# A fused retention and squared-ReLU feed-forward kernel: the last group of tokens moved to the seven-product form and woven into the group in front, and one operand sum rebuilt from another

## The chip, the cores and the metric

The kernel runs on one core of one Trainium2 chip. The metric is device time in microseconds (us) for one execution. The engines are written as in the profile: PE (matrix multiply), PEld (its weight load, which runs ahead of the multiply), DVE (vector), ACT (scalar and activations), POOL (GpSimd), SP (the queue that issues nearly all DMAs).

## What is computed

The reference, cut to what matters:

```python
B, H, S, D = 8, 8, 576, 64             # q, k, v: [B, H, S, D] float32
scores = q @ k.T / sqrt(D)
ret    = (scores * Dmat) @ v           # Dmat: gamma_h ** (i - j) for i >= j, else 0
x      = ret.transpose(0, 2, 1, 3).reshape(B * S, 512)   # 4608 tokens x 512
h      = x @ w_in                      # w_in  512 x 2048
g      = relu(h) ** 2
out    = g @ w_out                     # w_out 2048 x 512, float32
```

## The kernel before

**Tiles and groups.** The 4608 tokens are 36 units of 128 tokens; two units make a group, so there are 18 groups, numbered 0 to 17 (`groups`, line 132 on). The last group holds its two units in reverse order. A unit is a chunk of 128 positions of one batch, or a "tail", the last 64 positions of two batches together.

**Stages of one unit.** k, q and v are loaded in float32 by DMA, cast to float16 by POOL, k and q are transposed (by PE for the first eight units, by DMA after), and the retention is worked out in 64 x 64 pieces on PE (`psc` scores, `psS` running sums, `psO` outputs). DVE writes the result as `xT`, the operand of the feed-forward part.

**Feed-forward of one group, first product** (`add_ff`, line 805 on). `ph = x @ w_in` comes in eight blocks of 8 matmuls of 128x256 (64 matmuls; 4 matmuls make one slice of 128 hidden features, and a block holds two slices). ACT takes each block through Relu into `rl` (line 827), then ACT (`SQ_ACT`: blocks 0 to 6) or DVE (block 7; in groups 0 and 1 all blocks) squares it into `gT` (lines 837, 839).

**Second product.** Groups 0, 1 and 17 use the plain form (line 860). The other fifteen (`STRASSEN = 2`) use `add_strassen` (line 878 on), Strassen's scheme in Winograd's form on 2 x 2 blocks: seven block products of 8 matmuls of 128x256 in place of eight, that is 56 matmuls in place of 64 such, or of 32 matmuls of 128x512. The four quarters of g are G(s, i): s is the unit (A or B), i the lower or upper half of the hidden features. DVE forms four sums in float16, each in two halves h0 and h1, into `gS` (line 890):

- S3 = G(A,0) - G(B,0), S1 = G(B,0) + G(B,1), S2 = S1 - G(A,0), S4 = G(A,1) - S2.

The order of the products on PE is P1, P7, P6, P2, P5, P3, P4. P7 reads S3, P6 reads S2, P5 reads S1, P3 reads S4; P1, P2, P4 read g itself. P1, P6, P5 and P3 add up in one PSUM bank "a", and ACT copies its state out after P1, P6 and P5 (line 925) and after P3 (line 955). P7 and P4 share bank "c". DVE adds the copies to banks and writes the output tile `o` (line 935). SP stores it.

**Names in the trace.** In rows of line 912 (all seven products) `po<-w_out,gT` is P1 or P2, `po<-wT,gS` is P7, P6 or P5, `po<-w_out,gS` is P3 and `po<-wT,gT` is P4. `wT` are differences of `w_out` blocks, made once by DVE (line 772).

**What sets the order.** All work is entered as tasks with an engine, a key, a duration and what it depends on (`Schedule`, line 16 on). `emit` walks through time with these durations, gives each free engine the ready task of the smallest key, and so fixes the order of the instructions on each engine once and for all. On the chip an engine works in this order and waits when an operand isn't there. The planner also counts buffers: `ff=4` PSUM banks for `ph` and `po`, `rl=3`, `u` buffers `p1`, `u2`, `u4` one each. Where `p6`'s operand is late in the plan, the planner puts first-product work of the next group ahead of it.

**Loads at the start.** `FIRST` gives the order of the first loads: pairs of units (`k0`, `q0`, ...) and eight weight blocks of 1 MB (`w0` to `w3` of w_in, `w4` to `w7` of w_out), one after the other on SP (`add_load_pair`, line 284; `add_weight`, line 295). The planner takes a load as landed 2.1 us after its slot ends.

**The end.** Group 17's plain second product is 16 matmuls of 128x512 for one unit, then 2 x 16 of 128x256 for the other. ACT copies each result out (line 869) and issues the stores itself (`store`, line 786).

Of the kernel before, what the change touches and what calls it, by code (L numbers as in the profile page):

```python
# [9 lines left out]
FP32 = mybir.dt.float32  # L10
FP16 = mybir.dt.float16
ACTF = mybir.ActivationFunctionType
ALU = mybir.AluOpType
# [88 lines left out]
def kernel(  # L102
# [9 lines left out]
    nc = tc.nc  # L112
    B, H, S, D = q.shape
    DM, DFF = w_in.shape
    assert (B, H, S, D, DM, DFF) == (8, 8, 576, 64, 512, 2048)
    P = 128
    NP = H // 2
    NF = DFF // P
# [13 lines left out]
    groups = []  # L132
# [16 lines left out]
    u_pool = ctx.enter_context(tc.tile_pool(name="u", bufs=1))  # L149
# [75 lines left out]
    SQ_ACT = (0, 1, 2, 3, 4, 5, 6)  # L225
    JOIN = 11
    PAIRED = 8
    FIRST = ["k0", "q0", "v0", "k2", "q2", "w0", "v2", "w1", "w2", "w3", "w4", "w5", "w6", "w7", "k4", "q4", "v4", "k6", "q6", "v6"]
    sched = Schedule(dict(ff=4, prS=1, prO=1, g=3, ld=5, wst=4, kq=7, v16=7, rT=4, x=3, rl=3, o=4, p1=1, u2=1, u4=1,
# [32 lines left out]
    def dma_task(key, dur, fn, **kw):  # L262
        t = add("SP", key, dur, fn, deps=list(last_load), **kw)
        last_load[:] = [t]
        return t
# [18 lines left out]
    def add_load_pair(name, u):  # L284
        b, c = units[u][1:]
        n = "kqv".index(name)

        def fn():
            if name != "q":
                tile_of["stage", u] = stage.tile([P, 2, H, 2 * D], FP32, name="pair", tag="wst")  # L290
            x = tile_of[name + "32", u] = tile_of["stage", u][:, n % 2]
            nc.sync.dma_start(out=x, in_=(k, q, v)[n][b, :, c * P:(c + 2) * P, :].rearrange("h (p e) d -> p h (e d)", e=2))
        loaded[name, u] = loaded[name, u + 1] = dma_task(0, 1.81 if loaded else 2.9, fn, acq=("wst",) if name != "q" else ())

    def add_weight(i):
# [10 lines left out]
        t = dma_task(0, 2.75, fn, acq=("wst",))  # L306
# [479 lines left out]
    def store(u, o, lo=0, hi=DM):  # L786
        kind, b, c = units[u]

        eng = nc.scalar if group_of[u] == len(groups) - 1 else nc.sync
        if kind == "full":  # L790
            r0 = b * S + c * P
            eng.dma_start(out=out[r0:r0 + P, lo:hi], in_=o[:, lo:hi])
        else:
            for i in range(2):
                r0 = (b + i) * S + 512
                eng.dma_start(out=out[r0:r0 + 64, lo:hi], in_=o[i * 64:(i + 1) * 64, lo:hi])
# [8 lines left out]
    def add_ff(g):  # L805
        us = groups[g]
        n = len(us)
        base = us[0] * L
# [3 lines left out]
        for fb in range(NF // nf):  # L812
            for j in range(nf):
# [7 lines left out]
                f1.append(add("PE", base + (nf * fb + j) * n, 0.01 + 0.2133 * n, f,  # L821
# [7 lines left out]
            on_act = n == 2 and g >= STRASSEN and fb in SQ_ACT  # L829
# [10 lines left out]
            r = add("ACT", base + 4 * fb + 4, 0.6, fr, deps=[f1[-1]], acq=("rl",))  # L840
            sched.free("ff", [r])
            sq.append(add("ACT" if on_act else "DVE", base + 4 * fb + 6, 0.63 if on_act else 0.45, fg, deps=[r] + sq[:1],
# [4 lines left out]
        if STRASSEN <= g < len(groups) - 1:  # L847
            add_strassen(g, us, base2, sq)
            return
        for s, u in enumerate(us):  # L850
            end = base2 + NF * (s + 1)
            f2 = T["ff2"][-1:] if s == 0 else f2[-1:]

            cuts = [(0, DM)] if u != groups[-1][-1] else [(0, HM), (HM, DM)]
            for ci, (lo, hi) in enumerate(cuts):
                for fi in range(NF):
                    def f(fi=fi, s=s, u=u, lo=lo, hi=hi):
                        if fi == 0:
                            tile_of["po", u, lo] = ps_ff.tile([P, hi - lo], FP32, name="po", tag="ff")
                        nc.tensor.matmul(tile_of["po", u, lo], lhsT=tile_of["g", g][:, fi, s * P:(s + 1) * P],  # L860
                                         rhs=w_out16[:, fi, lo:hi], start=(fi == 0), stop=(fi == NF - 1))
                    f2.append(add("PE", base2 + NF * s + fi / len(cuts) + 8 * ci, 0.0025 + 0.2135 / len(cuts), f,
                                  deps=[sq[fi // nf]] + wcast[4 + fi // 4] + f2[-1:],
                                  acq=("ff",) if fi == 0 else ()))

                def fo(u=u, lo=lo, hi=hi):
                    if lo == 0:
                        tile_of["o", u] = o_pool.tile([P, DM], FP32, name="o", tag="o")
                    nc.scalar.copy(out=tile_of["o", u][:, lo:hi], in_=tile_of["po", u, lo])
                oc = add("ACT", end + 1, 0.12 + 0.47 / len(cuts), fo, deps=[f2[-1]], acq=() if lo else ("o",))  # L870
                sched.free("ff", [oc])
                st = add(*(("ACT", end + 1.1, 0.05) if g == len(groups) - 1 else ("SP", -0.5, 0.7)),
                         lambda u=u, lo=lo, hi=hi: store(u, tile_of["o", u], lo, hi), deps=[oc], after=2.5)
            sched.free("o", [st])
# [3 lines left out]
    def add_strassen(g, us, base, sq):  # L878
        uA, uB = us
# [20 lines left out]
        s1 = add_sum(0, base, lambda h: G(1, 0, h), lambda h: G(1, 1, h), ALU.add, lambda h: low(h) + high(h) + s3[:1])  # L900
        s2 = add_sum(1, base + 1, lambda h: Sx(0, h), lambda h: G(0, 0, h), ALU.subtract, lambda h: [s1[h]])
        s4 = add_sum(3, base + 4, lambda h: G(0, 1, h), lambda h: Sx(1, h), ALU.subtract, lambda h: [s2[h]])
# [36 lines left out]
        p1 = product(1, 0, "a", raw(0, 0), wB[0, 0], low, True, True, [])  # L939
        c1 = on_act_copy("p1", "a", 5, [p1])  # L940
        p7 = product(7, 4, "c", summed(2), wT[2], lambda h: [s3[h]], True, True, [])
        p6 = product(6, 8, "a", summed(1), wT[1], lambda h: [s2[h]], False, True, [c1])
        c2 = on_act_copy("u2", "a", 13, [p6])
        p2 = product(2, 12, "b", raw(0, 1), wB[1, 0], high, True, True, [])
        d11 = on_dve_add(uA, 0, "b", "p1", 17, [p2, c1], ("o",))
        sched.free("ff", [d11])
        sched.free("p1", [d11])
        p5 = product(5, 16, "a", summed(0), wT[0], lambda h: [s1[h]], False, True, [c2])
        c4 = on_act_copy("u4", "a", 21, [p5])
        d22 = on_dve_add(uB, 1, "c", "u4", 22, [p7, c4], ("o",))  # L950
        sched.free("u4", [d22])
        p3 = product(3, 20, "a", summed(3), wB[1, 1], lambda h: [s4[h]], False, True, [c4])

        def f12():
            nc.scalar.copy(out=o_tile(uA)[:, HM:], in_=bank("a"))
        c12 = add("ACT", base + 25, 0.37, f12, deps=[p3, d11])
        sched.free("ff", [c12])
        p4 = product(4, 24, "c", raw(1, 1), wT[3], high, False, True, [d22])
        d21 = on_dve_add(uB, 0, "c", "u2", 29, [p4, d22])
        sched.free("ff", [d21])  # L960
        sched.free("u2", [d21])
# [3 lines left out]
        for u, ds in ((uA, [d11, c12]), (uB, [d22, d21])):  # L965
            st = add("SP", -0.5, 0.7, lambda u=u: store(u, o_tile(u)), deps=ds, after=2.5)
            sched.free("o", [st])
# [44 lines left out]
```

## Time and profile before

| what | value |
|---|---|
| five runs | 297.94, 297.97, 298.6, 299.36, 299.38 us; median 298.6 |
| the profiled execution | 297.97 us, of which the span of the trace is 296.2 us |
| granted PE clock | 1.000 over the span |
| DVE busy | 195.1 us (66%) |
| ACT busy | 187.3 us (63%) |
| POOL busy | 93.3 us (32%) |
| first-product matmuls, line 819 | 1152 |
| seven-product matmuls, line 912 | 840 |
| plain second-product matmuls, line 860 | 112 |

The span is the time from the first to the last instruction of the trace; 1.8 us of the execution lie outside it. A busy PE is a PE with a matmul in its pipeline; consecutive matmuls overlap, so a count of instructions times their mean duration gives more than the time they take. The pace of a stretch is better read from its first and last start. The runs shown lie within 0.5%.

### The profile page before, as it was taken

Reading aid. Unit: us, or ns where it says so; the run is one execution under the profiler, and the core shown is the slowest. Engines: PE = TensorE matmul, PEld = TensorE weight load, DVE = VectorE, ACT = ScalarE, POOL = GpSimd, SP = SyncE. Lnnn points to the kernel's source line nnn. Section 1 sums busy time; section 2 is a strip of 40 time slices with the busy share of each in tenths; the row PEclk is TensorE's granted clock in tenths of the full one; section 3 lists DMA queues with packets and bytes.
Section 4 is the critical chain, followed back from the end, with each engine's and each line's share of the span. In section 5 each row is a group of like instructions: output and inputs, shape, how many; then the busy total and the mean of one; then the engine's idle time right before and its main releaser. Section 6 shows DMA issues by size and latency. Waiting matters only on the chain.

```text
span 296.2 us, 10048 instructions
## 1 busy us (share of the span) xinstructions
PE 286.1 (97%) x4320; PEld 233.8 (79%) x4320; DVE 195.1 (66%) x413; ACT 187.3 (63%) x354; POOL 93.3 (32%) x129
## 2 busy tenths in 40 slices
PE   8989989999999999999999999999999999999995
PEld 3558745688878888888888888788888888888874
DVE  3777469869395949493959597766786767462410
ACT  5357753484867676748576667656666666658861
POOL 4453384434242415063414153414141520000000
PEclk9999999999999999999999999999999999999999
DMA  7999999999999999899979699999898980101012
GB/s 201 326 371 385 363 261 236 195 208 167 209 166 213 178 194 171 203 213 220 163 172 165 156 187 223 201 176 197 155 215 144 216 156 10 73 3 71 2 71 73
DMA packets 139262, 54.14 MB, mean 183 GB/s; under 512 B 118097, under 2 KB 130641, under 8 KB 139217
## 3 DMA queue, kind: packets, MB, share of 16 engines
q1 hardware_dynamic: 138768, 52.97, 86.0%
q8 instruction: 34, 0.56, 0.8%
q10 hardware_dynamic: 448, 0.52, 0.6%
q14 instruction: 12, 0.09, 0.1%
HBM read 36.70 MB, written 9.44 MB: 156 GB/s over the span
## 4 chain that ended last, share of the span: by engine, by line
PE 68%; DVE 10%; ACT 10%; DMA 6%; issue 2%; POOL 2%; POOLq 0%
PE po L912 27%; PE ph L819 26%; ACT rl L827 5%; DVE gS L890 5%; PE psO L337 4%; ACT gT L837 4%; PE po L860 4%; DMA wo<-in_moe_w_out_dram 3%; PE warm L241 3%; DMA pair<-in_k_dram 3%; DVE gT L839 2%; PE psc L337 1%; PE psS L337 1%; PE psT L412 1%; POOL qx L397 1%
## 5 line engine op out<-in xcount | busy, mean ns | idle before, releaser
L819 PE MATMUL ph<-xT,w_in 128*128 128x256 f16 x1152 | 139.3, 273 | 0.0
L819 PEld LDWEIGHTS <-w_in 128*128 128x128 f16 x1152 | 111.2, 98 | 14.8 <-POOL w_in L316 0.3
L827 ACT ACTIVATE rl<-ph 128x512 f16<-128x512 f32 x144 | 84.0, 588 | 52.0 <-PE ph L819 49.1
L837 ACT ACTIVATE gT<-rl 128x512 f16<-128x512 f16 x112 | 70.5, 630 | 3.5
L890 DVE TENSOR_TENSOR gS<-gT 128x512 f16<-128x512 f16 x60 | 31.1, 519 | 40.4 <-ACT gT L837 39.8
L912 PEld LDWEIGHTS <-gS 128*128 128x128 f16 x480 | 45.7, 98 | 9.3 <-DVE gS L890 3.8
L912 PE MATMUL po<-wT,gS 128*128 128x256 f16 x360 | 49.2, 273 | 1.6 <-DVE gS L890 1.2
L361 POOL TENSOR_TENSOR v<-v,vdec_full 128x512 f16<-128x512 f32 x24 | 25.6, 1068 | 56.8 <-DMA v<-in_v_dram 53.8
L912 PEld LDWEIGHTS <-gT 128*128 128x128 f16 x360 | 34.8, 98 | 4.4 <-issue 0.2
L912 PE MATMUL po<-w_out,gT 128*128 128x256 f16 x240 | 31.1, 273 | 0.0
L349 POOL CAST kq<-k 128x512 f16<-128x512 f32 x28 | 19.1, 681 | 34.6 <-DMA k<-in_k_dram 25.6
L839 DVE TENSOR_TENSOR gT<-rl 128x512 f16<-128x512 f16 x32 | 17.7, 555 | 14.2 <-ACT rl L827 13.9
L349 POOL CAST kq<-q 128x512 f16<-128x512 f32 x28 | 18.2, 648 | 26.5 <-DMA q<-in_q_dram 26.1
L860 PE MATMUL po<-w_out,gT 128*128 128x512 f16 (+1 forms) x112 | 22.6, 349 | 0.3 <-POOL w_out L316 0.3
L698 DVE TENSOR_TENSOR xT<-psO,gam_full 128x512 f16<-128x512 f32 x28 | 18.4, 684 | 3.4 <-PE psO L337 3.3
L925 ACT COPY u<-po 128x256 f32<-128x256 f32 x30 | 11.0, 367 | 14.5 <-PE po L912 14.4
L935 DVE TENSOR_TENSOR o<-po,u 128x256 f32<-128x256 f32 x30 | 12.5, 418 | 11.3 <-PE po L912 7.7
L637 DVE TENSOR_TENSOR rT<-psc,mask 128x512 f16<-128x512 f32 x28 | 18.5, 681 | 1.3 <-PE psc L337 1.3
L860 PEld LDWEIGHTS <-gT 128*128 128x128 f16 x112 | 10.6, 98 | 8.1 <-issue 0.5
L890 DVE TENSOR_TENSOR gS<-gT,gS 128x512 f16<-128x512 f16 x30 | 16.3, 546 | 1.0
L890 DVE TENSOR_TENSOR gS<-gS,gT 128x512 f16<-128x512 f16 x30 | 15.8, 527 | 1.0
L912 PE MATMUL po<-wT,gT 128*128 128x256 f16 x120 | 15.8, 273 | 0.2 <-DVE o L935 0.2
(78 smaller groups left out, 263.9 us busy)
## 6 DMA issues: line engine op xcount, KB each, us to landing
out_dram<-o SPq DMA_DIRECT2D x31, 256.0 KB, 3.1
k<-in_k_dram SPq DMA_DIRECT2D x24, 256.0 KB, 4.6
q<-in_q_dram SPq DMA_DIRECT2D x24, 256.0 KB, 5.0
v<-in_v_dram SPq DMA_DIRECT2D x24, 256.0 KB, 4.7
wi<-in_moe_w_in_dram SPq DMA_DIRECT2D x4, 1024.0 KB, 9.9
wo<-in_moe_w_out_dram SPq DMA_DIRECT2D x4, 1024.0 KB, 9.6
pair<-in_k_dram SPq DMA_DIRECT2D x4, 512.0 KB, 4.2
pair<-in_q_dram SPq DMA_DIRECT2D x4, 512.0 KB, 7.3
```

The costliest lines, as they stand in the source:

```text
L337: nc.tensor.matmul(out_, lhsT=lhsT, rhs=rhs, start=start, stop=True, skip_group_check=True, tile_position=(64 * row, 64 * col))
L349: op(out=out_.rearrange("p (n b a d) -> p n b a d", n=2, b=2, a=2), in_=in_.rearrange("p (n a b) d -> p n b a d", n=2, a=2))
L361: nc.gpsimd.tensor_tensor(out=t, in0=tile_of["v32", u], in1=vdec[kind].rearrange("p (h o) -> p h o", o=1).to_broadcast([P, H, D]), op=ALU. ...
L637: nc.vector.tensor_tensor(out=r, in0=tile_of["psc", g][:, :, cols(s)].rearrange("p a (n i) -> p a n i", i=64), in1=mask.rearrange("p (o r ...
L698: nc.vector.tensor_tensor(out=tile_of["x", g][:, :, s * P:(s + 1) * P].rearrange("p n (c i) -> p c n i", c=2), in0=tile_of["psO", g][:, :, ...
L819: nc.tensor.matmul(tile_of["ph", g, fb][:, j, :], lhsT=w_in16[:, m, fi * P:(fi + 1) * P], rhs=tile_of["x", g][:, m, :], start=(m == 0), st ...
L827: nc.scalar.activation(out=t, in_=tile_of["ph", g, fb], func=ACTF.Relu)
L837: nc.scalar.activation(out=t, in_=rl, func=ACTF.Square)
L839: nc.vector.tensor_tensor(out=t, in0=rl, in1=rl, op=ALU.mult)
L860: nc.tensor.matmul(tile_of["po", u, lo], lhsT=tile_of["g", g][:, fi, s * P:(s + 1) * P], rhs=w_out16[:, fi, lo:hi], start=(fi == 0), stop= ...
L890: nc.vector.tensor_tensor(out=Sx(k, h), in0=in0(h), in1=in1(h), op=op)
L912: nc.tensor.matmul(tile_of["pb", g, bank], lhsT=left(i), rhs=right[:, i, :], start=(start and i == 0), stop=(i == HF - 1), skip_group_chec ...
```

## The change

Three things are changed.

1. **S2 from S3.** S2 is now G(B,1) - S3, which is the same value as S1 - G(A,0). It depends on S3 and the upper half, no longer on S1. In the order of the keys S2 comes ahead of S1. This holds for all groups with seven products.
2. **The last group.** Group 17 also uses seven products. Its first product gets keys that put it ahead of the second product of group 16. Its P1, P6, P5, P3 (one quarter of the output) go in parts of two matmuls among the products of group 16 where the planner finds room, and P2, P7, P4 come last. P4 has a bank of its own ("e"), and P7 is first added to a copy (new line 966). Four stores of 128x256 take the place of three: those of d11 and d22 are issued by ACT, those of c12 and d21 by SP. In groups 16 and 17 only blocks 1, 4 and 6 are squared by ACT (`SQ_LATE`), the other five by DVE. The `u` buffers become two each.
3. **The plan's times for four loads.** `LAG` tells the planner that v2, w1, k4, q4 land 1.2, 1.3, 0.7 and 0.5 us later than it assumed. The order of the loads stays; the order of other work on the engines moves.

```diff
-    u_pool = ctx.enter_context(tc.tile_pool(name="u", bufs=1))
+    u_pool = ctx.enter_context(tc.tile_pool(name="u", bufs=2))
...
+    SPREAD = 0.1
+    SQ_LATE = (1, 4, 6)
+    LAG = {"v2": 1.2, "w1": 1.3, "k4": 0.7, "q4": 0.5}
-    sched = Schedule(dict(... p1=1, u2=1, u4=1, ...
+    sched = Schedule(dict(... p1=2, u2=2, u4=2, ...
...
-        loaded[...] = dma_task(0, 1.81 if loaded else 2.9, fn, acq=...)
+        loaded[...] = dma_task(0, 1.81 if loaded else 2.9, fn, acq=..., after=2.1 + LAG.get(name + str(u), 0.0))
-        t = dma_task(0, 2.75, fn, acq=("wst",))
+        t = dma_task(0, 2.75, fn, acq=("wst",), after=2.1 + LAG.get(f"w{i}", 0.0))
...
-        base = us[0] * L
+        base = min(us) * L
+        def place(x):
+            return base + x if g < last_g else base - NF * n - 1 + SPREAD * x
...
-            on_act = n == 2 and g >= STRASSEN and fb in SQ_ACT
+            on_act = g >= STRASSEN and fb in (SQ_ACT if g < last_g - 1 else SQ_LATE)
...
-        if STRASSEN <= g < len(groups) - 1:
+        if STRASSEN <= g:
             add_strassen(g, us, base2, sq)
...
-        s1 = add_sum(0, base, ... G(1, 0, h), ... G(1, 1, h), ALU.add, low(h) + high(h) + s3[:1])
-        s2 = add_sum(1, base + 1, ... Sx(0, h), ... G(0, 0, h), ALU.subtract, [s1[h]])
-        s4 = add_sum(3, base + 4, ...)
+        early = 12 if g == last_g else 0
+        s2 = add_sum(1, base - 4 - early, ... G(1, 1, h), ... Sx(2, h), ALU.subtract, high(h) + [s3[h]])
+        s1 = add_sum(0, base + 1 - early, ... G(1, 0, h), ... G(1, 1, h), ALU.add, low(h) + high(h) + s3[:1])
+        s4 = add_sum(3, base + 4 - early, ...)
...
+        if g == last_g:
+            last[:] = []
+            at = -2 * NF * n
+            p1 = product(1, at + 3.5, "a", raw(0, 0), wB[0, 0], low, True, True, [])
+            c1 = on_act_copy("p1", "a", at + 8, [p1])
+            p6 = product(6, at + 11.5, "a", summed(1), wT[1], lambda h: [s2[h]], False, True, [c1])
+            c2 = on_act_copy("u2", "a", at + 16, [p6])
+            p5 = product(5, at + 19.5, "a", summed(0), wT[0], lambda h: [s1[h]], False, True, [c2])
+            c4 = on_act_copy("u4", "a", at + 24, [p5])
+            p3 = product(3, at + 27.5, "a", summed(3), wB[1, 1], lambda h: [s4[h]], False, True, [c4])
+            c12 = add("ACT", base + 1, 0.37, f12, deps=[p3], acq=("o",))
+            p2 = product(2, 12, "b", raw(0, 1), wB[1, 0], high, True, True, T["ff2"][-1:])
+            d11 = on_dve_add(uA, 0, "b", "p1", 17, [p2, c1, c12])
+            p7 = product(7, 16, "c", summed(2), wT[2], lambda h: [s3[h]], True, True, [])
+            p4 = product(4, 24, "e", raw(1, 1), wT[3], high, True, True, [])
+            d22 = on_dve_add(uB, 1, "c", "u4", 21, [p7, c4], ("o",))
+            d7 = add("DVE", base + 22, 0.42, f7, deps=[d22, c2], acq=("p1",))
+            d21 = on_dve_add(uB, 0, "e", "p1", 29, [p4, d7])
+        else:
...
```

The order of the instructions in the two programs, as the planner fixes it. From the end of P4 of group 15 on, PE has work worth 228 matmuls of 128x256 in the kernel before (a matmul of 128x512 counted as two) and 224 in the changed one; of this, four first-product matmuls of group 16 stood ahead of that point before. Between P7 and the second half of P6, the first-product matmuls that PE has are, for groups 2 to 15: before 12, 12, 12, 12, 12, 12, 12, 12, 20, 16, 16, 16, 12, 12; after 16, 8, 8, 8, 16, 8, 8, 8, 12, 16, 12, 12, 16, 8 (in group 13 with scores and part of the retention outputs of the next group among them). In the first 40 us, eight of the 128 first-product matmuls of groups 0 and 1 move behind the cast of the last weight block. On SP, the loads of the first 60 us keep their order among themselves.

## The prediction

> **What bounds the kernel now.** I read the page first: PE is busy over nearly the whole span, no other engine over 66%.
>
> ```profile
> span 296.2 us, 10048 instructions
> PE 286.1 (97%) x4320; PEld 233.8 (79%) x4320; DVE 195.1 (66%) x413; ACT 187.3 (63%) x354; POOL 93.3 (32%) x129
> ```
>
> The timeline of PE and PEld then gives the pace. From 268.05 us, 44 first-product matmuls take until the next group starts at 272.85: 0.109 us each, and a product of 8 takes 0.87 us. One matmul of 128x512 costs two of these (16 from 285.95, the next half at 289.4). From 262.4 us to the end no row of PE or PEld shows a wait: the end is matmuls, back to back, then one copy and one store. Each work item taken off PE there is time saved.
>
> ```profile
> 285.95 7.11 PE L860 MATMUL po<-w_out,gT 128*128 128x512 f16 x48
> ...
> 291.54 0.37 ACT L869 COPY o<-po 128x256 f32<-128x256 f32 x1 [1.35 <-PE po L860]
> ...
> 293.10 0.37 ACT L869 COPY o<-po 128x256 f32<-128x256 f32 x1 [1.19 <-PE po L860]
> 293.50 0.34 ACTq L792 DMA_DIRECT2D out_dram<-o  x1
> ```
>
> Where does PE wait earlier? The list of waits has one entry that the change touches:
>
> ```profile
> PEld L912 <- DVE gS L890: 3.8, 8, 0.7
> ```
>
> Eight waits of P6 for S2. In the weight-load timeline they stand at 83.00 (0.52 us), 128.01 (0.35), 143.36 (0.58), 187.88 (0.74), 189.43 (0.34), 203.84 (0.50), 218.74 (0.42) and 233.60 (0.38), 3.83 us in all, in groups 3, 6, 7, 10 (twice), 11, 12, 13. PE never makes these up, since everything behind it is dense. The vector timeline of group 7 shows the chain that ends in one:
>
> ```profile
> 140.86 0.43 DVE L839 TENSOR_TENSOR gT<-rl 128x512 f16<-128x512 f16 x1
> 141.32 1.24 DVE L890 TENSOR_TENSOR gS<-gT 128x512 f16<-128x512 f16 x1
> 142.60 0.71 DVE L890 TENSOR_TENSOR gS<-gS,gT 128x512 f16<-128x512 f16 x1
> ```
>
> Square of block 7, then S1, then S2 of half h1, ending 143.31; P6's second half loads at 143.36.
>
> **Part 1, S2 from S3.** It removes S1 from in front of S2; DVE's work stays the same. The price of the removed step: an undisturbed sum takes 0.43 us (median of the rows of line 890), but here it took 1.24, since POOL's v multiply ran from 141.24 to 142.28. This is where the Trainium skill speaks against the change: *SBUF — State Buffer*, "Who interferes with whom", says that a vector instruction with two SBUF inputs is shut out by a GpSimd instruction that reads SBUF, for the whole of that instruction, if that began first. So the delay belongs to POOL's instruction and not to S1: S2, now first, would pay it instead. By the row, S2 is earlier by what S1 took: 1.24 us in group 7, 1.15 in group 6. By the rule S2 now ends about where S1 ended (142.56), earlier by only what S2 itself took: 0.71 us, or 0.43 where POOL is quiet. I take the rule's reading.
>
> Against that: the planner knows S2 is earlier and puts first-product work that filled the gap elsewhere. In groups 3, 7, 10, 12 and 13 PE comes to the second half of P6 with four to eight matmuls fewer since P7, 0.44 to 0.87 us sooner; in group 6 four more; in group 11 as many. Per wait, saved = wait - max(0, wait + sooner - S2's gain):
>
> - group 3: S1 ended at 81.76, S2 at 82.95 (1.15 us); wait 0.52 gone but for some 0.05: saves 0.45
> - group 6: four matmuls more, S2 0.72 earlier: saves 0.35
> - group 7: 0.44 sooner, 0.71 earlier, 0.58 - 0.27 left: saves 0.27
> - group 10: first wait, S2 0.45 to 1.15 earlier but less work in front; second 0.43 earlier; of 1.08 I take 0.4 as saved
> - group 11: same work, 0.43 earlier: saves 0.43
> - group 12: 0.44 sooner, 0.43 earlier: saves 0
> - group 13: scores and outputs of the next group (about 0.9 us) now lie in front: saves 0.38
>
> Sum 2.3 (0.45 + 0.35 + 0.27 + 0.4 + 0.43 + 0.38). The groups without a wait had little or much in hand (S2 ends at 98.11 for a load at 98.16 in group 4, at 112.07 for 112.94 in group 5); with PE 0.44 sooner and S2 0.43 earlier they keep it. I take off 0.3 for small new waits: **2.0 us**, with 0 (each saved gap planned away) and 3.8 (all gone) as the ends. S1 and S4 come later by one step, 0.43 to 0.71 us; P5 and P3 read them one product (0.87) or more behind P6, so that is covered; without P2 in between it would cost its length.
>
> **Part 2, the last group.** 56 matmuls of 128x256 take the place of 64 such: 8 x 0.109 = **0.87 us** off PE, if PE stays dense. I checked the new order with the durations of the rows, T being the end of group 15's P4. All first-product work and P1 of group 16 end by T+13.1. ACT then carries 14 Relus (0.59) and 5 squares (0.63), 11.4 us, in the 12 us from T+1.0: behind by at most 0.7 us; last Relu done at T+13.7, copy of P1 of group 16 at T+14.1. P6 of 16 starts at T+14.8: a reserve of 0.7 us. The last S2 of group 17 needs block 7's square (DVE, T+14.2) and is there at T+14.6; P6's second half at T+16.6. The copies of bank "a" of the two groups alternate, so each (0.37, plus about 0.1 from PE) lies beside 0.87 us or more of the other group's product. Taking squares to DVE costs nothing: 10 x 0.43 + 16 sums x 0.43 + 8 adds x 0.42 = 14.5 us of DVE in 25, and POOL's last row is before 250. Banks: with P1's held, the first product turns over three; block k waits for the Relu of block k-3, done 0.5 us or more ahead. If ACT were over 0.7 us later than this, PE would wait by the excess.
>
> The last step: DVE's add (0.42) for ACT's copy (0.37), +0.05; SP, not ACT, issues the store after a hand-over, about +0.1; SP's stores of 128 KB took a median 2.5 us to land, ACT's 1.7, but SP's ran beside loads and these do not: between 0 and 0.8, I take 0.1. The added d7 follows d22 (0.42 each) after P7 and ends with P4, 0.87 us after P7: 0 to 0.1 more. Splitting the stores in halves puts two more DMAs on the queues, both beside P7 and P4. So the end gains 0.87 - 0.05 - 0.1 - 0.1, **0.6 us**.
>
> **Part 3, the first 60 us.** The loads keep their order and arrive as before, so PE meets the same arrivals with its work in another order. Before, the outputs of group 1 (`psO`, 23.2 us) stood behind 12 first-product matmuls of w1; now they stand behind four. Eight others move ahead of the sums (`psS`) that wait for v2, into PE's 1.34 us before 19.46; but w1's cast ends at 21.73 in any order, and PE had only warm-up matmuls to do up to there, so this gains nothing. At 24 us PE has done 20 first-product matmuls, not 28, and is about 0.35 us ahead for it: 0.5 us behind. It then waits some 0.75 us for w4's cast (29.95), and when w7's is there (38.26) it has eight matmuls, 0.87 us, to do that were done before. What can take them up is idle time that PE had behind that:
>
> ```profile
> 38.32 2.32 PE L860 MATMUL po<-w_out,gT 128*128 128x512 f16 x10 [0.33 <-POOL w_out L316]
> ...
> 41.16 0.40 PE L412 MATMUL psT<-ident,kx 128*128 128x128 f16 x4 [0.30 <-POOL kx L397]
> ...
> 49.06 0.30 PE L337 MATMUL psO<-kqT,R 64*64 64x128 f16 x4 [0.19 <-DVE rx L455]
> ```
>
> The weight loads are idle 0.47 and 0.68 us before the last two and 0.28 before 43.19, 1.4 us in all, most of which the 0.87 us can fill. At 49 us PE waits for DVE's masks, so the time up to there is DVE's. Price: **+0.2 us**; ends -0.6 (the idle time gone) and +1.2 (0.87 in full and a new wait of 0.3).
>
> **Sum.** -2.0 - 0.6 + 0.2 = -2.4 us. The profiled execution took 297.97 (span 296.2), so 295.6 by its own time. It is at the low end of its five runs; from their median, 298.6, the forecast is **296.2 us**.
>
> **The rivals.**
>
> *The planner takes the gain back.* S2 is earlier by 0.43 and PE is sent to it earlier by 0.44, as in group 12, in most groups. For it: ten of the groups 2 to 15 have fewer matmuls in the gap. Against it: four of the seven waiting groups keep the work or get more, or gain over 0.44. Then only -0.6 + 0.2 remain: 298.2, chance 0.23.
>
> *Slower: POOL's multiply falls on S2.* The nine groups with less work in the gap (all those but 13, where scores take its place) have PE there 0.44 us or more sooner. If POOL's v multiply (1.04 us, two to a group of 14.9 us) hits the square of block 7 or S2 there, that is a wait of about 0.6 us: the square took 1.04 instead of 0.43 at 216.43. For it: five of the present waits (81.46, 125.86, 141.24, 186.28, 216.15) have such a row in front, and loads and casts now move against DVE. Against it: S2 stands only one step behind the square now, so fewer steps can be hit. It decides from waits of 5.1 us in all (3.83 + 0.6 - 0.2 + 0.9), 0.37 per group where it is 0.27 now. With 0.6 in the nine and 0.2 in the other five it is 6.4: 298.6 + 2.6 - 0.4 = 300.8. Chance 0.14.
>
> *The end doesn't hold.* ACT is some 1.3 us later than worked out at T+14, so that P6 waits 0.6 us and the gain of the end is gone: 296.8. Chance 0.09.
>
> **Numbers.** Forecast 0.54 (its own range 294.6 to 297.5), taken back 0.23, slower 0.14, end not held 0.09. A difference under 0.3%, 0.9 us, can't be told from none. Faster by more: the forecast but 0.02, the whole last case, a quarter of the second, 0.66. Within: 0.02 and most of the second, 0.19. Slower: the third and 0.01 of the second, 0.15. The low end, 294.4, is 3.8 at P6 and 0.6 at the end with the start as it was, 298.6 - 4.4 = 294.2, nearly in full; the high end, 299.3, takes in the second case with the start at its +1.2 (299.2) and leaves out the slower one, 0.14, and little else.
>
> **What would show it.** Right: PEld's waits for gS fall from 3.8 us to about 1.5; PE is dense behind the last first-product matmul; the last store is issued about 0.6 us after DVE's last add starts. Wrong: waits for gS in groups 3, 7, 10 or 12 as long as now, or new ones with a POOL row on the square or S2; waits of P6 for ACT's copies in the last 12 us; group 2's P1 later than its 63.6 us by more than 0.5.

## The result, and the profile after

The changed kernel takes **297.22 us** (median of 31 runs), the kernel before 298.68 (52 runs); the ratio is 0.9961 with a 95% interval of 0.9949 to 0.9974. That is 1.2 us (0.8 to 1.5) by the ratio, half of the 2.4 that were forecast. The profiled execution of the changed kernel took 297.33 us, at its median; that of the kernel before, 297.97, had been 0.7 under its own. So the two traces differ by less (0.6 us of span) than the medians.

The page of the changed kernel, span and busy times:

```profile
span 295.6 us, 10076 instructions
...
PE 285.8 (97%) x4328; PEld 235.0 (80%) x4328; DVE 204.1 (69%) x433; ACT 183.2 (62%) x347; POOL 94.6 (32%) x129
```

DVE has 9 us more to do, PE nearly the same busy time. The list of waits of the changed kernel (engine, tile and line that waited, what ended the wait: total us, times, longest), the entries of the seven products that end with DVE:

```profile
PEld L914 <- DVE gS L891: 1.9, 6, 0.6
...
PE po L914 <- DVE o L937: 0.9, 3, 0.5
...
PE po L914 <- DVE gS L891: 0.4, 1, 0.4
```

The first entry was 3.8 us, eight times. It fell by 1.9, as forecast. The second is new: P4 waits three times for d22, the add that reads P7 out of the bank that P4 adds to. Group 7 shows how the one became the other. DVE's timeline of the changed kernel (start, us, engine, line, operation):

```profile
141.27 0.42 DVE L891 TENSOR_TENSOR gS<-gT,gS 128x512 f16<-128x512 f16 x1
141.61 1.26 DVE L891 TENSOR_TENSOR gS<-gT 128x512 f16<-128x512 f16 x1
142.80 0.82 DVE L891 TENSOR_TENSOR gS<-gT,gS 128x512 f16<-128x512 f16 x1
...
147.10 1.10 DVE L670 TENSOR_TENSOR R<-stmp,dec 128x256 f16<-128x256 f32 x1
148.13 0.41 DVE L937 TENSOR_TENSOR o<-po,u 128x256 f32<-128x256 f32 x1
```

POOL's:

```profile
141.43 1.16 POOL L365 TENSOR_TENSOR v<-v,vdec_full 128x512 f16<-128x512 f32 x1 [0.81 <-PE psS L341]
...
146.88 1.04 POOL L365 TENSOR_TENSOR v<-v,vdec_full 128x512 f16<-128x512 f32 x1 [1.91 <-DMA v<-in_v_dram]
```

And PE's, with its idle time in brackets:

```profile
148.59 1.03 PE L914 MATMUL po<-wT,gT 128*128 128x256 f16 x8 [0.49 <-DVE o L937]
```

S2 (141.27) is now first and short; S1 behind it takes 1.26, beside POOL's multiply of v. P6 no longer waits. But DVE then works without a break to d22 at 148.13, with a second multiply (146.88) on the last step of R, 1.10 in place of 0.42. In the kernel before, the two rows were

```profile
148.06 0.41 DVE L935 TENSOR_TENSOR o<-po,u 128x256 f32<-128x256 f32 x1
...
148.76 1.05 PE L912 MATMUL po<-wT,gT 128*128 128x256 f16 x8
```

so PE came to P4 after d22 had ended. Now PE is there at 148.10, and waits for a d22 that is as late as it was.

The end of the changed kernel, timeline of all engines:

```profile
291.71 0.41 DVE L966 TENSOR_TENSOR p<-po,u 128x256 f32<-128x256 f32 x1
...
292.23 0.42 DVE L937 TENSOR_TENSOR o<-po,p 128x256 f32<-128x256 f32 x1
292.68 0.34 SPq L794 DMA_DIRECT2D out_dram<-o  x1
```

The last result is ready at 292.65, where the copy had ended at 293.47; SP's hand-over costs 0.03 us. The store then needs 2.9 us to the end of the span, where ACT's needed 2.7. Over the sixteen traces of this document, it is 2.94 to 3.07 us behind SP's last store (nine kernels) and 2.68 to 2.70 behind ACT's (seven).

**Where the time went.** The trace is cut in three at instructions that stand behind the same work in all kernels: the first matmul of P1 of group 2 and of group 15. A **loss** is the time from the start of one matmul to the start of the next, less the median of that time for the same kind of matmul; it is counted where it is over 0.06 us, between these two points. Losses at P6 are for S2 or the sums near it, at P4 for d22, at R for the masked sums that the retention outputs read. The 0.1 that PE loses at each switch to or from retention work, in every kernel, is left out. The three stretches are up to the P1 of group 2, from there to the P1 of group 15, and from there to the end of the span. All in us, from one profiled execution each; e1 to e14 are explained below.

| kernel | ratio to before, 95% | P1 of group 2 | to P1 of 15 | to the end | P6 | P4 | R |
|---|---|---|---|---|---|---|---|
| before | 1 | 63.62 | 195.10 | 37.47 | 2.90 | 0.31 | 0 |
| after | 0.9961 (0.9949 to 0.9974) | 63.89 | 194.75 | 36.97 | 1.18 | 1.16 | 0.16 |
| e1_p1_only | 0.9934 (0.9911 to 0.9958) | 63.61 | 194.58 | 37.46 | 2.15 | 0 | 0.67 |
| e2_p1_held | 0.9896 (0.9865 to 0.9927) | 63.36 | 193.37 | 37.47 | 0.33 | 1.09 | 0 |
| e3_p2_only | 0.9982 (0.9963 to 1.0001) | 63.57 | 196.19 | 37.03 | 3.55 | 0.61 | 0.12 |
| e4_p3_only | 0.9991 (0.9977 to 1.0004) | 63.91 | 194.65 | 37.47 | 2.72 | 0 | 0 |
| e5_p2_own | 0.9990 (0.9972 to 1.0008) | 63.59 | 195.96 | 36.99 | 3.96 | 0 | 0.08 |
| e6_held_own | 0.9887 (0.9861 to 0.9913) | 63.68 | 192.80 | 36.99 | 0.43 | 0.48 | 0 |
| e7_after_held | 0.9874 (0.9844 to 0.9904) | 64.01 | 192.80 | 37.05 | 0 | 0.37 | 0.54 |
| e8_held_vcopy | 0.9859 (0.9829 to 0.9889) | 63.69 | 191.82 | 37.46 | 0 | 0 | 0 |
| e9_after_vcopy | 0.9871 (0.9850 to 0.9893) | 63.82 | 192.09 | 37.10 | 0.25 | 0 | 0 |
| e10_held_vcopy2 | 0.9863 (0.9843 to 0.9884) | 63.73 | 191.92 | 37.07 | 0 | 0 | 0 |
| e11_d22_lag | 0.9931 (0.9909 to 0.9954) | 63.87 | 193.00 | 36.97 | 0.52 | 0 | 0.57 |
| e12_held_d22_lag | 0.9879 (0.9858 to 0.9899) | 63.72 | 192.82 | 36.99 | 0.59 | 0 | 0.29 |
| e13_before_vcopy | 0.9866 (0.9827 to 0.9905) | 63.87 | 192.37 | 37.48 | 0.52 | 0 | 0 |
| e14_before_s2lat | 0.9924 (0.9902 to 0.9947) | 64.32 | 192.65 | 37.48 | 0.07 | 0.78 | 0 |

For the changed kernel the columns read: 1.72 us less at P6, 0.85 more at P4 and 0.16 more at R, so 0.71 less by these; the stretch is 0.35 shorter. The other 0.36 is three steps inside the retention work, which no column has: 0.17 in group 6, where an output at 132.26 follows DVE's masked scores `rT` (ended at 132.21), and 0.11 at 81.17 and 0.08 at 239.22, whose cause is open.

The columns come from single executions, which can lie off their kernel's median: e11's 1.25 us under it, that of e4 and of the kernel before 0.7 under, those of e1 and e3 0.4 over. They show what was waited for; what a kernel costs is read from the ratios.

### The profile page after: what moved, and what is told of

Its sections match the earlier page's. It is cut to its first block, busy times and chain, and to the rows that moved or that the text cites. A ratio compares the mean times of both kernels' runs of the same rounds, so it can differ in the third digit from the quotient of the medians.

```text
span 295.6 us, 10076 instructions
## 1 busy us (share of the span) xinstructions
PE 285.8 (97%) x4328; PEld 235.0 (80%) x4328; DVE 204.1 (69%) x433; ACT 183.2 (62%) x347; POOL 94.6 (32%) x129
## 4 chain that ended last, share of the span: by engine, by line
PE 78%; DVE 8%; DMA 6%; ACT 3%; SPq 2%; issue 2%; POOL 0%; DVEq 0%
PE ph L825 36%; PE po L914 30%; PE po L863 5%; DMA wi<-in_moe_w_in_dram 3%; PE psO L341 3%; DMA wo<-in_moe_w_out_dram 3%; DVE gS L891 2%; SPq L295 2%; PE psc L341 2%; PE psS L341 1%; ACT gT L843 1%; DVE o L937 1%; ACT rl L833 1%; DVE rT L641 1%; DVE stmp L666 1%
## 5 line engine op out<-in xcount | busy, mean ns | idle before, releaser
L843 ACT ACTIVATE gT<-rl 128x512 f16<-128x512 f16 x104 | 65.6, 631 | 3.0
L914 PEld LDWEIGHTS <-gS 128*128 128x128 f16 x512 | 49.1, 98 | 7.7 <-DVE gS L891 1.9
L891 DVE TENSOR_TENSOR gS<-gT,gS 128x512 f16<-128x512 f16 x64 | 38.0, 596 | 21.4 <-ACT gT L843 20.8
L914 PE MATMUL po<-wT,gS 128*128 128x256 f16 x384 | 52.2, 273 | 0.4 <-DVE gS L891 0.4
L891 DVE TENSOR_TENSOR gS<-gT 128x512 f16<-128x512 f16 x64 | 33.4, 522 | 20.5 <-ACT gT L843 20.5
L914 PEld LDWEIGHTS <-gT 128*128 128x128 f16 x384 | 37.3, 98 | 5.4 <-issue 0.9
L914 PE MATMUL po<-w_out,gT 128*128 128x256 f16 x256 | 34.5, 273 | 0.0
L914 PE MATMUL po<-w_out,gS 128*128 128x256 f16 x128 | 16.6, 273 | 0.0
L863 PE MATMUL po<-w_out,gT 128*128 128x512 f16 x64 | 15.6, 379 | 0.5 <-POOL w_out L320 0.4
L670 DVE TENSOR_TENSOR R<-stmp,dec 128x256 f16<-128x256 f32 x24 | 13.3, 553 | 0.7
```

The source lines that it names most:

```text
L843: nc.scalar.activation(out=t, in_=rl, func=ACTF.Square)
L863: nc.tensor.matmul(tile_of["po", u], lhsT=tile_of["g", g][:, fi, s * P:(s + 1) * P], rhs=w_out16[:, fi, :], start=(fi == 0), stop=(fi == N ...
L891: nc.vector.tensor_tensor(out=Sx(k, h), in0=in0(h), in1=in1(h), op=op)
L914: nc.tensor.matmul(tile_of["pb", g, bank], lhsT=left(i), rhs=right[:, i, :], start=(start and i == 0), stop=(i == HF - 1), skip_group_chec ...
```

## The experiments

Two theories stood at first for the missing half. A: DVE's chain is late in any order, and what P6 saves is waited for at d22. B: the planner saw the earlier S2 and spent it.

**Each part alone.**

e1, part 1 in the kernel before:

```diff
-        s1 = add_sum(0, base, ... G(1, 0, h), ... G(1, 1, h), ALU.add, ...)
-        s2 = add_sum(1, base + 1, ... Sx(0, h), ... G(0, 0, h), ALU.subtract, lambda h: [s1[h]])
+        s2 = add_sum(1, base - 4, ... G(1, 1, h), ... Sx(2, h), ALU.subtract, lambda h: high(h) + [s3[h]])
+        s1 = add_sum(0, base + 1, ... G(1, 0, h), ... G(1, 1, h), ALU.add, ...)
```

> The kernel before with part 1 alone (S2 from S3, with its key). The prediction: -2.0 us, as P6's waits for S2 go. Theory A (DVE is what is late): DVE works without a break from the squares through the three sums to d22, its work is no shorter, and what PE saves at P6 it waits for at P4 (for d22) or for R: about -0.4 us, the weight loads' waits for gS down by 2 us and P4's waits for DVE's o up by 0.8. Theory B (the planner): also about -0.4 us, but because first-product work was moved away from in front of P6 and P4; the two are told apart by the next kernel.

e2, the same sums, but the planner isn't told: S2 takes S1's slot, S1 takes that of S2, and in the plan P6 waits for the second slot:

```diff
-        s1 = add_sum(0, base, ...)
-        s2 = add_sum(1, base + 1, ...)
+        s2 = add_sum(1, base, ... G(1, 1, h), ... Sx(2, h), ALU.subtract, lambda h: low(h) + high(h) + [s3[h]])
+        s1 = add_sum(0, base + 1, ... G(1, 0, h), ... G(1, 1, h), ALU.add, lambda h: [s2[h]])
...
-        p6 = product(6, 8, "a", summed(1), wT[1], lambda h: [s2[h]], False, True, [c1])
+        p6 = product(6, 8, "a", summed(1), wT[1], lambda h: [s1[h]], False, True, [c1])
```

> The kernel before, and only the two sums change places on DVE: S2 (from S3) in the slot of S1, S1 in the slot of S2, with the planner told that P6 waits for the second slot as before, so that PE and ACT keep the order of the kernel before to the last instruction. Theory B: nothing is planned away, the waits at P6 go and nothing comes in their place: -1.5 to -2.0 us, P4's waits for d22 as before (one, group 3, 0.3 us at the matmuls). Theory A: P6's waits shrink from 2.9 to about 1.0 us at the matmuls, but P4 in groups 3 and 7 comes earlier to a d22 that is as late as before and waits 0.3 to 0.6 us in each: -0.9 us or less.

e3, part 2 alone (in the changed kernel, S2 from S1 again and LAG empty):

```diff
-    LAG = {"v2": 1.2, "w1": 1.3, "k4": 0.7, "q4": 0.5}
+    LAG = {}
...
-        s2 = add_sum(1, base - 4 - early, ... G(1, 1, h), ... Sx(2, h), ...)
+        s2 = add_sum(1, base + 1 - early, ... Sx(0, h), ... G(0, 0, h), ... lambda h: [s1[h]])
```

> The kernel before with part 2 alone (last group in seven parts, S2 from S1 as before, no LAG). The prediction and the trace of after: -0.6 us, all behind the last group of scores. Rival: the end only holds because S2 is early there too; then P6 of the last group waits for S2 and 0.3 us or more of it is lost.

e4, part 3 alone (in the kernel before, the table and its two uses):

```diff
+    LAG = {"v2": 1.2, "w1": 1.3, "k4": 0.7, "q4": 0.5}
...
-        t = dma_task(0, 2.75, fn, acq=("wst",))
+        t = dma_task(0, 2.75, fn, acq=("wst",), after=2.1 + LAG.get(f"w{i}", 0.0))
```

> The kernel before with part 3 alone (the planner is told later landings for four loads). The prediction: +0.2 us (ends -0.6 and +1.2). Theory A and B: +0.2 to +0.3 at the P1 of group 2, which may be lost in the waits of the groups behind it: 0 to +0.3.

Measured: part 1 alone 2.0 us (0.66%), with the order held 3.1 us (1.04%); parts 2 and 3 can't be told from none by their times. With the order held, group 7 of e2 on DVE:

```profile
140.68 0.42 DVE L890 TENSOR_TENSOR gS<-gT,gS 128x512 f16<-128x512 f16 x1
141.02 1.26 DVE L890 TENSOR_TENSOR gS<-gT 128x512 f16<-128x512 f16 x1
...
146.51 1.20 DVE L666 TENSOR_TENSOR R<-stmp,dec 128x256 f16<-128x256 f32 x1
147.63 0.41 DVE L935 TENSOR_TENSOR o<-po,u 128x256 f32<-128x256 f32 x1
```

and on POOL:

```profile
140.73 1.27 POOL L361 TENSOR_TENSOR v<-v,vdec_full 128x512 f16<-128x512 f32 x1 [0.70 <-PE psS L337]
```

Both theories missed. P4's losses did rise, from 0.31 to 1.09 (groups 3, 7 and 12), as A says; but P6's fell to 0.33, where A had 1.0, and the time fell by more than B's 1.5 to 2.0. The prediction's -2.0 for part 1 was met by e1's times, but by luck: its trace has 0.75 us less at P6 and 0.67 more at R, not 2.3 less and 0.3 more. The rival named for e3 falls: without the early S2 its end is as short (37.03) as the changed kernel's (36.97). By the traces e1 saves only 0.5 us up to group 15, and e3 seems to cost 1.1 there. That rests on one execution of the kernel before, and e5 shows what it is worth.

The parts don't add up. The three ratios multiply to 0.9907, and the whole change has 0.9961: 1.6 us more, 0.6 to 2.7 by the intervals. Together with LAG and the second buffers, the planner makes another order of the early S2 in groups 2 to 15 than in e1, and it loses more. No run has part 1 with only one of the other two, so which of them brings this is open.

**The same order once more, and sums of parts.** In e3 the second `u` buffers could have let the planner order groups 2 to 15 anew. e5 gives the last group buffers of its own:

```diff
-    sched = Schedule(dict(..., p1=2, u2=2, u4=2,
+    sched = Schedule(dict(..., p1=1, u2=1, u4=1, p1L=1, u2L=1, u4L=1,
...
-            return add("ACT", base + key, 0.37, f, deps=deps, acq=(name,))
+            return add("ACT", base + key, 0.37, f, deps=deps, acq=(name + ("L" if g == last_g else ""),))
```

> Part 2 alone again, but the last group's copies u2, u4 and p1 have buffers of their own, so that the groups in front keep one each, as in the kernel before: PE, ACT and DVE then have the order of the kernel before up to group 16. Theory B (the planner: the second buffers let it order groups 2 to 15 anew, and that cost e3_p2_only 1.1 us there): from the P1 of group 2 to that of group 15 as before, 195.1 us, the end 0.5 us shorter, time -0.6 us or a little more. Theory A (only DVE's chain counts, the order does not): the same as e3_p2_only, -0.5 us, and 196 us from the P1 of group 2 to that of group 15.

Measured: 0.9990, and 195.96 us up to the P1 of group 15, not 195.10. From e5's list of waits:

```profile
PEld L914 <- DVE gS L891: 5.0, 9, 0.8
...
PE po L914 <- DVE gS L891: 2.4, 8, 0.6
```

By the names in the traces, PE, ACT, DVE and POOL run groups 2 to 15 of e5 in the order of the kernel before, and those of e3 too: the second buffers alone had changed nothing there. So one order took 195.10, 196.19 and 195.96 us in three executions, and lost 2.90, 3.55 and 3.96 us at P6. B's reading of e3 falls. A's figures were met (196 us, a time like e3's), but there was no other order to compare, so this says nothing for A. The profiled execution of the kernel before was a lenient one, which closes most of the gap between the times (1.2 us by the ratio) and the spans (0.6).

e6 is e5 with the sums of e2:

> Parts 1 and 2 without any reordering in groups 2 to 15: the two sums change places on DVE as in e2_p1_held, the last group has its own buffers as in e5_p2_own, no LAG. Theory B: the gains add, -2.9 - 0.6 = -3.5 us, 295.2. Theory A: the sum is less, as DVE's chain is late in any order: -2.0 us or less.

Measured: 3.4 us by the ratio, the gains of e2 and of the end together, as B expected.

e7 is the changed kernel with LAG and two buffers each, in which only the planner is kept from seeing S2 early (as in e2, for groups 2 to 16):

```diff
-        s2 = add_sum(1, base - 4 - early, ..., lambda h: high(h) + [s3[h]])
-        s1 = add_sum(0, base + 1 - early, ..., lambda h: low(h) + high(h) + s3[:1])
+        if g < last_g:
+            s2 = add_sum(1, base, ..., lambda h: low(h) + high(h) + [s3[h]])
+            s1 = add_sum(0, base + 1, ..., lambda h: [s2[h]])
+            s2, s1 = s1, s2
```

> The changed kernel, but in groups 2 to 16 S2 takes the slot of S1 and S1 that of S2, and the planner is told that P6 waits for the second slot: it plans PE as if S2 were as late as it was, with the changed kernel's buffers and LAG. Theory B as 'what is planned away is lost': S2 is 0.4 us or more ahead of its plan in each group, P6's waits at the matmuls fall to 0.5 us or less, and the time is 1 to 2 us under the changed kernel, about 295.5 to 296.2. Theory C (any new order is a new draw, and before's happened to be a good one): P4's waits for d22 stay at 1 us or come in other groups, and the time stays at that of the changed kernel, 297.2.

Measured: 0.9874, 0.87% under the changed kernel's 0.9961; 295.47 us against 297.22. The waits of the seven products in e7:

```profile
PE psO L341 <- DVE stmp L666: 0.5, 1, 0.5
...
PEld L920 <- DVE gS L891: 0.3, 2, 0.2
```

No matmul of P6 loses over 0.06 us. By the names in the traces, PE and ACT run groups 2 to 15 of e7 in the order of e4, with four more first-product matmuls (0.44 us) between P7 and P6's second half than in the changed kernel in ten groups. From the end of S2's second half to that half of P6 there are 0.27 us in the changed kernel (median of groups 2 to 14) and 1.02 in e7; it is 0.14 in e1 and 0.74 in e2. Group 8 shows what this is worth. In the changed kernel POOL's multiply began at 156.86, and S2 behind it took 1.26:

```profile
156.92 1.26 DVE L891 TENSOR_TENSOR gS<-gT,gS 128x512 f16<-128x512 f16 x1
158.10 0.82 DVE L891 TENSOR_TENSOR gS<-gT 128x512 f16<-128x512 f16 x1
```

PE was there and lost 0.17 at P6 and 0.33 at P4. In e7 the multiply (156.56) fell on S4, behind S2 and S1:

```profile
156.20 0.42 DVE L891 TENSOR_TENSOR gS<-gT,gS 128x512 f16<-128x512 f16 x1
156.54 0.42 DVE L891 TENSOR_TENSOR gS<-gT 128x512 f16<-128x512 f16 x1
156.87 1.26 DVE L891 TENSOR_TENSOR gS<-gT,gS 128x512 f16<-128x512 f16 x1
```

Neither loss is there. P6's second half began 1.19 us behind S2, so a hit on S2 (0.84 us) would have fitted in. One trace can't part this slack from where the multiply happened to fall: S2's second half was hit in five groups of the changed kernel's trace and in none of e7's. The times can: all five runs of e7 (295.07 to 295.57) lie under the fastest of the changed kernel's 31 (295.62).

This is theory B: the same sums, about as long on the chip (0.54 us on average, 0.56 in the changed kernel), and a plan that isn't allowed to count on S2. Theory C (a mere new draw) doesn't fit: from e4 to e7, with PE's order the same, the ratio falls by 1.17% with the end in it, as it did by 1.04% from the kernel before to e2; and e2, e6 and e7, held in two orders, lie at 0.9874 to 0.9896, while e1 and the changed kernel, which count on S2, lie at 0.9934 and 0.9961.

**Why a plan that uses the earlier S2 loses it.** The planner counts 0.45 us for a sum. Theory D: its order would do if sums took that, but behind POOL's multiply they take up to 1.29. Theory E: the order is too eager in any case. Four kernels replace the multiply of v by its decay (1.04 us, two inputs) by a cast, without changing the order of PE, ACT and DVE; their outputs lack that decay for the units from 8 on.

```diff
-            nc.gpsimd.tensor_tensor(out=t, in0=tile_of["v32", u], in1=vdec[kind]..., op=ALU.mult)
+            nc.gpsimd.tensor_copy(out=t, in_=tile_of["v32", u])
```

On e2:

> e2_p1_held with POOL's multiply of v by its decay (1.04 us, two SBUF inputs) replaced by a cast of v (one input) in units from 8 on; the decay of v is left out of the output. PE, ACT and DVE keep their order. If the remaining waits (P4 for d22 in groups 3 and 7, P6 in group 10, 1.4 us at the matmuls) come from DVE's two-input operations being held up to 1.27 us while POOL multiplies, DVE's rows of 1.15 to 1.27 us fall to 0.8 or less, these waits fall under 0.6 us, and the time is 0.5 to 1.0 us under e2_p1_held. If DVE is late by its own work, the waits stay over 1 us and the time within 0.3 us.

On the changed kernel:

> The changed kernel, in its own order on every engine, with POOL's multiply of v by its decay replaced by a cast in units from 8 on (the decay of v is left out of the output). Theory D (the planner's new order is only too tight for operations on DVE that last 1.15 to 1.27 us beside POOL's multiply where it counts 0.45): without the multiply the order is good, the remaining waits of P6 and P4 (2.3 us at the matmuls in groups 2 to 14) fall under 0.8, and the time is 2 us or more under the changed kernel, near 295. Theory E (the order loses by itself, PE being sent to P6 and P4 too soon in any case): waits of 1.5 us or more stay, and the time is 1 us or less under it.

On e7:

> e7_after_held with the same cast in place of POOL's multiply (the decay of v is left out of the output). Theory D: little is left to gain, 0.3 to 1.0 us under e7_after_held, so that it and e9_after_vcopy differ by 0.7 us or less where with the multiply they differ by 1.75. Theory E: the difference of 1.75 us stays.

On the kernel before:

> The kernel before, in its own order, with the cast in place of POOL's multiply of v in units from 8 on (the decay of v is left out of the output). If part 1 is worth its 2.9 us (with the order held) because POOL's multiply fell on the chain square, S1, S2: P6's waits (2.9 us and more at the matmuls) fall under 1.5 and the time is 2 us or more under before, so that part 1 is worth 1.5 us or less without the multiply. If part 1 is worth it because S1 is one step (0.43 us) in front of S2 in any case: P6's waits stay over 2 us and the time is 1 us or less under before.

Measured, as ratios to the kernel before:

| | with the multiply | with the cast |
|---|---|---|
| before | 1 | 0.9866 |
| e2, sums changed, order held | 0.9896 | 0.9859 |
| after | 0.9961 | 0.9871 |
| e7, after with the order held | 0.9874 | 0.9863 |

Theory D holds in both pairs: 1.04% and 0.87% apart with the multiply, 0.07% and 0.08% without, where the intervals (about 0.5% and 0.3% each way) can't tell them apart. e8 gained a little more on e2 than expected, 1.1 to 1.2 us. The groups of instructions say why. The changed kernel's (line, engine, operation, count, busy us, mean ns, idle before):

```profile
L891 DVE TENSOR_TENSOR gS<-gT,gS 128x512 f16<-128x512 f16 x64 | 38.0, 596 | 21.4 <-ACT gT L843 20.8
...
L365 POOL TENSOR_TENSOR v<-v,vdec_full 128x512 f16<-128x512 f32 x24 | 26.2, 1092 | 63.6 <-DMA v<-in_v_dram 61.6 <-PE psS L341 2.0
```

and e9's:

```profile
L889 DVE TENSOR_TENSOR gS<-gT,gS 128x512 f16<-128x512 f16 x64 | 31.5, 494 | 21.7 <-ACT gT L841 21.1
...
L365 POOL CAST v<-v 128x512 f16<-128x512 f32 x28 | 18.8, 671 | 65.5 <-DMA v<-in_v_dram 47.0 <-PE psc L341 8.4 <-PE po L912 6.5
```

The mean of these sums (S2 and S4) falls by 0.10 us. More to the point, 16 squares and sums of the changed kernel last over 0.95 us, and one in e9. e9's waits of P6 for the sums:

```profile
PEld L912 <- DVE gS L889: 0.5, 2, 0.2
```

e13 settles another point. Without the multiply, the kernel before with S1 still ahead of S2 has

```profile
PEld L910 <- DVE gS L888: 0.9, 3, 0.3
```

in place of 3.8. So S1's own 0.43 us was hardly ever what P6 waited for. It was POOL's multiply on the chain square, S1, S2, and part 1 is worth much only as a way out of it. The forecast counted a multiply in front of five of the old waits; the rows of the kernel before have one in all seven groups, in 11, 12 and 13 on the square. Group 11:

```profile
201.26 1.04 POOL L361 TENSOR_TENSOR v<-v,vdec_full 128x512 f16<-128x512 f32 x1 [6.87 <-DMA v<-in_v_dram]
...
201.46 1.12 DVE L839 TENSOR_TENSOR gT<-rl 128x512 f16<-128x512 f16 x1 [0.28 <-ACT rl L827]
```

The cast is also shorter than the multiply; these runs don't separate its length from its number of inputs.

**Slack in the plan alone.** If the plan is short of slack at P6, it may be so at P4. e11 adds to the changed kernel

```diff
+            d22["lat"] = 0.8
```

> The changed kernel, and the planner is told that d22 (the add that P4 waits for) is there 0.8 us after its end instead of 0.12; nothing else is edited. If a plan with slack at the consumer is what is missing at P4 too: P4's waits for d22 (groups 3, 7 and 8, 1.15 us at the matmuls) go, P6's stay at 1.2, and the time is 0.5 to 1.0 us under the changed kernel. If the slack only moves the wait: P6's or R's waits rise by as much, time within 0.3 us.

and e12 adds to e11

```diff
+        for t in s2:
+            t["lat"] = 0.6 if g < last_g else t["lat"]
```

> The changed kernel, with the planner told that S2 is there 0.6 us after its end and d22 0.8 us (the first alone gives the order of e7_after_held). If both help: 0.2 to 0.5 us under e7_after_held, 295.0 to 295.3, with no wait of P6 or P4 over 0.1 us at the matmuls. If not: at or above 295.5, with the first-product work that now stands in front of P4 missing elsewhere.

Measured: e11 has no loss for d22 left; 0.57 came up at R. By the medians it is 0.4 us under the changed kernel, by the ratios 0.9, with intervals that overlap: in or just under the range of the first expectation. Its traced execution was its fastest, so these losses are rather too small. e12 is the same as e7 within the interval (0.9879 and 0.9874), its P6 losing 0.59 (in group 2) where e7's R loses 0.54 (in group 5). Its median, 295.09, is where the first expectation had it; its losses at P6 are not. Past one slack, the next only moves the rest.

e14, the last run, gives the slack to the kernel before, with S2 still behind S1 (`t["lat"] = 0.6` for S2, nothing else):

> The kernel before with S2 still from S1, and only the planner told that S2 is there 0.6 us after its end instead of 0.12. If slack in the plan is all that is needed against the stretched operations, part 1 is not: P6's losses (3.1 to 4.2 us) fall under 1, and the time is 2 to 3 us under before. If S2 has to be early as well (behind S1 it is one step of 0.4 to 1.2 us later than the slack covers, or PE has no other work for the time): P6's losses stay over 1.5 us or come elsewhere, and the time is 1.3 us or less under before.

Measured: 0.9924, 2.3 us (1.6 to 2.9). P6's losses are 0.07; P4's rose to 0.78. One number in the plan, without a line of the change, gives more than the change does. e7 gives 0.5% more than that, with the end and both the early S2 and the slack; the intervals just touch.

No run tried a planner that knows POOL's multiply and counts 1.2 us where it falls.

## Why the prediction was half right

- **P6's waits.** The forecast was 2.3 us saved at the weight loads of the eight old waits; 2.46 went there, and with new waits in groups 2 and 8 the total fell from 3.83 to 1.86. In single groups the forecast was off. Groups 3, 7, 11 and 13 lost their waits whole. Group 10 gave 0.11 of 0.4: the multiply hits S2's first half in both kernels (1.15 and 1.29 us), and PE comes with eight matmuls fewer.
- **The step that failed is the term "I take off 0.3 for small new waits".** New ones are 0.85 at P4 (1.16 against 0.31), 0.17 at P6 in group 8, 0.10 in group 2, 0.16 at R in group 7 and 0.17 at `rT` in group 6: 1.45 us. The sum at the matmuls is 1.99 saved at the old waits, less 1.45, less 0.19 of open cause: the 0.35 of the table (about 0.9 by the ratio, since the traced execution of the kernel before was lenient). The reasoning asked what is late next only inside the chain of sums (S1 for P5, S4 for P3), not what stands behind it on DVE in one unbroken run: R and d22. The mechanism was named under the rival "the planner takes the gain back". It was given 0.23 and seen at P6 alone, from the count of matmuls in front of P6. e7 shows that it was this: 0.87% come back when the planner is kept from counting on S2. The truth lay between the forecast and that rival.
- **The size of the prize was mis-sized too.** The 3.83 us came from one lenient execution (5.0 in e5), and idle weight loads count more than PE loses: 3.83 there are 2.90 at the matmuls. With the order held, part 1 is worth 3.1 us (e2), not 2.0.
- **Rule against row.** The forecast took the Trainium skill, *SBUF — State Buffer*, "Who interferes with whom", to mean that S2 would pay POOL's delay in S1's place. The section makes it depend on which instruction begins first, and so do the rows. In group 7, S2 began 0.05 us ahead of the multiply in e2 (140.68 and 140.73) and 0.16 ahead in the changed kernel, and took 0.42 both times; S1 paid. In group 8 of the changed kernel the multiply began 0.06 us ahead, and S2 took 1.26. Over the sixteen traces, of the sums that overlap one multiply of v and no other work of POOL, all 93 that began first took 0.41 to 0.43 us; of the 38 that began second, 31 took longer, up to 1.30, and the other seven began within 0.02 us of the multiply or in its last 0.2. So neither reading holds everywhere. In the changed kernel S2 did pay in group 10 (first half) and in groups 2, 3, 5, 8 and 12 (second half, 1.15 to 1.26 us), as the forecast had it; in group 7 it got past the multiply and gained the whole stretched S1, the reading that was set aside.
- **The end, -0.6.** 37.47 to 36.97: -0.50. PE has no idle weight load over 0.06 us behind 262 us, so ACT's and DVE's reserves held. SP's hand-over was 0.03, as ACT's had been, where 0.1 more was forecast; the landing cost 0.2 for 0.1. In all nine traces with the new end this stretch is 36.97 to 37.10, in the seven with the old one 37.46 to 37.48. The times of e3 and e5 agree with this, but can't tell it from none.
- **The start, +0.2.** P1 of group 2 came 0.27 later. Over the profiled executions, seven kernels with LAG have it at 63.85 on average and nine without at 63.70; the spread within the nine is 63.36 to 64.32. The time of e4 can't be told from the kernel before. So the +0.2 is neither shown nor refuted.
- **Slower by POOL's multiply on S2 (0.14).** The hits came, but P6's second half lost 0.10, 0.17 and 0.10 by them (groups 2, 8 and 12), not 0.6 in nine groups. **The end doesn't hold (0.09):** it held.

## What to carry to other kernels

When a list planner fixes the order with fixed durations, an operand made earlier is worth its lead only if the plan doesn't spend it: change the data dependence with the order frozen first, then let the plan see it, and compare. Put the slack where the measured durations exceed the planned ones (here 0.45 planned, up to 1.29 measured); one latency in the plan (e14) did more than the change. And when a wait on an engine's result goes, walk down that engine's queue to the next result that the waiting engine needs.

## What was not expected of the hardware

- The same order of PE, ACT, DVE and POOL took 195.10, 196.19 and 195.96 us over groups 2 to 15 in three executions, with 2.90, 3.55 and 3.96 us lost at P6. Which of DVE's sum and POOL's multiply begins first decides how long a sum is: 0.05 us to one side or the other makes it 0.42 or 1.26 us long.
- The stretching goes both ways: where DVE's sum began first (e2, 140.68), the multiply took 1.27 us in place of 1.04.
- A cast on POOL, with one input, stretches DVE's sums too: the 21 sums of e9 over 0.5 us all overlap a cast, and take 0.71 to 0.88 us.
